# Direct tiles and last projections as floating filler in a convolution pipeline on TensorE

## The chip, the cores and the metric

One Trainium2 chip, one of its cores. The metric is the device time of one execution in microseconds (us). A dilated causal convolution with a gate and an output projection is computed; every engine runs a fixed list of instructions in order, made at build time by a small list scheduler inside the kernel, from modelled durations.

TensorE is PE in the profile (PEld: its weight loads), VectorE is DVE, ScalarE is ACT, SyncE is SP (it issues the DMAs).

## The reference, cut to what matters

```python
B, T, D, K = (2, 16000, 144, 15)        # x [2,16000,144], w [15,144,288], w_o [144,144], all bf16
h = sum over i in 0..14 of  xp[:, pad - 2*i : pad - 2*i + T, :] @ w[i]     # dilation 2, causal
z = tanh(h[..., :144]) * sigmoid(h[..., 144:])
return z @ w_o
```

## The kernel before: the parts that matter

Time is cut into 128 segments of 250 steps; a "tile" is one step of all 128 segments. The first ten tiles are "direct": 15 matmuls over the first 128 channels, 2 over the other 16, that is 17 a tile. All the others come in 30 "units", which share sums and differences between taps: VectorE prepares differences, TensorE multiplies (items named S, X, V, Y, D), ScalarE copies partial sums inside PSUM and from PSUM to SBUF, VectorE adds them, the D matmuls finish the sum in PSUM, ScalarE applies tanh and sigmoid, VectorE multiplies (Z), a transposing DMA and a projection follow. In what follows D of unit n is its first D matmul, WA,DD in the profile.

Inputs of the units are staged: an engine copies them into one of two staging buffers (STA by VectorE, STB by ScalarE) and a DMA transposes that into XA or XB.

```python
NST = 2                                          # staging buffers
def load_xb(o):                                  # 16 remaining channels of eight tiles
    for h in range(2):
        g.add("act", <copy XBc -> STB[:, q, half h]>, w=[("STB", q, h)], dur=0.5, prio=2)      # q = o % NST
    g.add("sp", <dma_start_transpose XB <- STB>, r=[("STB", q, 0), ("STB", q, 1)], w=[("XB", s)], dma="xb", ...)
```

The scheduler models a DMA as landing DMA_LAT = 2.3 us after its bytes have passed at 280 kB per us. The scheduler hands out the eight banks of PSUM, the memory that TensorE writes its sums to, and it does so in the program's order:

```python
asks = [op for op in self.ops if op.alloc]       # every operation that wants a bank
def banks(op):
    if op is not asks[ai[0]]:                    # not its turn: wait
        return None
    ...
```

`prio` orders operations that could start at the same time (a smaller number goes first), and an operation is never placed before those in `soft`. An operation on TensorE that is "floating" may be pulled out of TensorE's program order when nothing else is ready; all others keep it. The direct tiles did not float. The last unit's odd tiles are not projected through a transposing DMA but by TensorE itself, in "ship pairs": four transposes into two banks, a copy by VectorE and one by ScalarE, four matmuls into a third bank, an eviction by ScalarE, a store.

```python
fill = [f for k in range(6, 10) for f in direct_parts(k)]
for f in fill[:FILL0]:                           # FILL0 = 20: all of them, before unit 0
    f()
...                                              # the 30 units
for o in (o0, o1):                               # the end
    project_some(o, (0, 2, 4, 6)); store_some(o, (0, 2, 4, 6), 2, 4, 0)
for dl in dls:                                   # four ship pairs, each with two stores
    ship_pair(o0, o1, dl)                        # transposes and projection floating=True
    for o in (o0, o1):
        store_some(o, (dl,), 2, 1, dl)
```

Of the kernel before, what the change touches and what calls it, by code (L numbers as in the profile page):

```python
# [72 lines left out]
class _Graph:  # L73
# [58 lines left out]
    def run(self, hint):  # L132
# [36 lines left out]

        asks = [op for op in self.ops if op.alloc]  # L170
        ai = [0]

        def banks(op):
            if op is not asks[ai[0]]:
                return None
            got, used = [], set()
            for bk in op.alloc:
                c = [b for b in range(0, 8, bk.n) if all(bopen[x] and x not in used for x in range(b, b + bk.n)) and (bk.pin is None or bk.pin == b)]
                if bk.n == 1:
                    c = [b for b in c if not bopen[b ^ 1] or (b ^ 1) in used] or c  # L180
                if not c:
                    return None
                b = min(c, key=lambda b: (max(bfree[b:b + bk.n]), b))
                used.update(range(b, b + bk.n))
                got.append(b)
            return got
# [5 lines left out]
        while n < len(self.ops):  # L192
# [39 lines left out]
            else:  # L232
                op.end = st + op.dur + TAIL[op.eng]
            ai[0] += 1 if op.alloc else 0
            for bk, b0 in zip(op.alloc, got or ()):
# [92 lines left out]
def _conv_wavenet_kernel(nc, x, w, w_o, out):  # L328
# [38 lines left out]
    BANK_O = 6  # L367
    FILL0 = 20
    LAG = 2
# [3 lines left out]
    with contextlib.ExitStack() as st:  # L373
# [368 lines left out]
        def finish(bk, z0, z1):  # L742
            s = ts_n[0] % NTS
            ts_n[0] += 1

            def th(a):
                return a.activation(TS[:, s, 0, :, :], both(bk, 0, D), ACT.Tanh)  # L747

            def sg(a):
                return a.activation(TS[:, s, 1, :, :], both(bk, D, D), ACT.Sigmoid)  # L750
            g.add("act", [th, sg], r=[bk], w=[("TS", s)], frees=[bk], dur=2 * t_act(2 * D), prio=0)

            def gt(v):
                dst = bass.AP(Z[:].tensor, (z0[0] * 8 + z0[1]) * D, [[NZ * 8 * D, NP], [((z1[0] - z0[0]) * 8 + z1[1] - z0[1]) * D, 2], [1, D]])
                return v.tensor_tensor(dst, TS[:, s, 0, :, :], TS[:, s, 1, :, :], ALU.mult)  # L755
            g.add("dve", gt, r=[("TS", s)], w=[("Z",) + z0, ("Z",) + z1], dur=t_tt(2 * D))

        wor_keys = [("WORp", dl, part) for dl in range(8) for part in range(2)]
# [3 lines left out]
        def ship_pair(o0, o1, dl):  # L762
# [9 lines left out]
            g.add("pe", fns, r=[("Z", zs[0], dl), ("Z", zs[1], dl), "ID"], alloc=[pa, pb], dur=0.24, floating=True)  # L772
            g.add("dve", lambda v: v.tensor_copy(zt(q, 0, 256), PSb[:, pa.b * 1024:pa.b * 1024 + 256]), r=[pa], w=[("ZTL", q, 0), ("Xr", 0)], frees=[pa], dur=0.21)
            g.add("act", lambda a: a.activation(zt(q, 256, 256)[0:DB, :], PSb[0:DB, pb.b * 1024:pb.b * 1024 + 256], ACT.Copy), r=[pb], w=[("ZTL", q, 1)], frees=[pb], dur=0.29)
            bo = _Bank()
            fns = []
            for i in range(2):
# [7 lines left out]
                                                PS[:, bo.b * 512:bo.b * 512 + 2 * D].rearrange("p (a b) -> p a b", a=2), ACT.Copy),  # L785
                  r=[bo], w=[("OS", s0, dl), ("OS", s1, dl)], frees=[bo], dur=t_act(2 * D))
            for s in (s0, s1):
                if s in last_store:
                    op.deps.add(last_store[s])

        def store_some(o, dls, step, n, d0):
            os_ = o % NO

            def f(e):
                src = bass.AP(OS[:].tensor, (os_ * 8 + d0) * D, [[NO * 8 * D, NP], [step * D, n], [1, D]])
                dst = bass.AP(out_t, (KD + 8 * o + d0) * D, [[L * D, NP], [step * D, n], [1, D]])
                return e.dma_start(dst, src)
            g.add("sp", f, r=[("OS", os_, d) for d in dls], w=[], dur=0.5, dma="st", nbytes=NP * n * D * 2)

# [8 lines left out]

        def project(o, gi):
            a, c = GROUPS[gi]  # L810
# [4 lines left out]
            for blk in range(a, c + 1):  # L815
# [3 lines left out]
                def f(t, q0=q0, n=q1 - q0 + 1, blk=blk, wi=wi, first=(blk == a)):  # L819
# [3 lines left out]
                fns.append(f)  # L823
            g.add("pe", fns, r=[("ZT", zt)] + wor_keys, alloc=[bk], dur=0.1255 + 0.1227 * (c - a - 1))
            op = g.add("act", lambda e: e.activation(OS[:, os_, a:c, :].rearrange("p e d -> p (e d)"), PS[:, bk.b * 512:bk.b * 512 + (c - a) * D], ACT.Copy),  # L825
                       r=[bk], w=[("OS", os_, d) for d in range(a, c)], frees=[bk], dur=t_act((c - a) * D), prio=1)
            if os_ in last_store:
# [10 lines left out]
        def project_some(o, dls):  # L838
            zt, os_ = o % NZT, o % NO
            for part in (dls[:2], dls[2:]):  # L840
                bk = _Bank()

                def mk(bk=bk, part=part):
                    out = []
                    for i, dl in enumerate(part):
                        for k in range(2):
                            out.append(lambda t, i=i, dl=dl, k=k: t.matmul(PS[:, bk.b * 512 + i * D:bk.b * 512 + i * D + D], lhsT=ZT[:, zt, dl + k, :], rhs=WOR[:, 2 * dl + k, :],
                                                                           start=(i == 0 and k == 0), stop=True, skip_group_check=True))
                    return out
                g.add("pe", mk(), r=[("ZT", zt)] + wor_keys, alloc=[bk], dur=0.063 * 2 * len(part))  # L850
                op = g.add("act", lambda e, bk=bk, part=part: e.activation(bass.AP(OS[:].tensor, (os_ * 8 + part[0]) * D, [[NO * 8 * D, NP], [2 * D, len(part)], [1, D]]),
                                                                           PS[:, bk.b * 512:bk.b * 512 + len(part) * D].rearrange("p (a b) -> p a b", a=len(part)), ACT.Copy),
                           r=[bk], w=[("OS", os_, d) for d in part], frees=[bk], dur=t_act(len(part) * D))
                if os_ in last_store:
                    op.deps.add(last_store[os_])
# [185 lines left out]

        def direct(k, b, pi, t0, t1):
            e = H + k
            g.add("pe", region(b, [(lambda e_=e - DIL * i: xa_tile(e_)) for i in range(t0, t1)], [(lambda i_=i: WA[:, i_, :]) for i in range(t0, t1)], t0 == 0),
                  r=[("XA", aslot(o)) for o in sorted(set(oct_of(e - DIL * i)[0] for i in range(t0, t1)))] + [("WA", pi)], dur=(t1 - t0) * MM, **({"alloc": [b.bk]} if t0 == 0 and k % 2 == 0 else {"w": [b.bk]}))

        def direct_b(k, b):
            e = H + k
            g.add("pe", region(b, [lambda: xb_tile(e), lambda: xb_tile(e - 2)], [lambda: WB[:, 0, :], lambda: WB[:, 1, :]]),
                  r=[("XB", bslot(-1)), ("XB", bslot(0)), ("WB", 0), ("WB", 1)], w=[b.bk], dur=2 * MM)  # L1050

# [5 lines left out]
        load_xchunk(0).deps.add(wa_op)  # L1057
        dp = [_Bank(2 * i if i < 3 else None, 2) for i in range(5)]
        db = [_Half(dp[k // 2], k % 2) for k in range(10)]
# [4 lines left out]
        for pi, (t0, t1) in enumerate(wa_pieces):  # L1064
            for k in range(6):
                direct(k, db[k], pi, t0, t1)
        for k in range(6):
            direct_b(k, db[k])
            if k % 2:
                finish(dp[k // 2], zdir(k - 1), zdir(k))  # L1070

        def direct_parts(k):
            out = [lambda pi=pi, t0=t0, t1=t1: direct(k, db[k], pi, t0, t1) for pi, (t0, t1) in enumerate(wa_pieces)]

# [5 lines left out]

        fill = [f for k in range(6, 10) for f in direct_parts(k)]
        for f in fill[:FILL0]:
            f()
        fill = fill[FILL0:]
        load_xa(1)
# [88 lines left out]
        todo_p = []  # L1174
        shipped = False
        for t in range(-reach, NUN):
# [4 lines left out]
            for name, off in pattern:  # L1181
# [11 lines left out]
                if not 0 <= u < NUN:  # L1193
                    continue
                if t < 0 and fill:
                    fill.pop(0)()
                if name[0] == "G":
# [4 lines left out]
                if name[0] == "D":  # L1202
# [6 lines left out]
                    elif done_d[u] == 4 and u == NUN - 2:  # L1209
                        for o in (o0, o1):  # L1210
                            ship(o, (0, 2, 4, 6))
            if fill and t == -1:
                for f in fill:
                    f()
                fill = []
            if not fill and not shipped:
                ship(-1, (6, 7))
                ship(0, range(8))
                shipped = True
        for x in todo:  # L1220
            project(*x[:2])
        m, r, o0, o1 = octs(NUN - 1)
        for o in (o0, o1):
            project_some(o, (0, 2, 4, 6))
            store_some(o, (0, 2, 4, 6), 2, 4, 0)
        dorder = [x for x, _ in pattern if x[0] == "D"]
        dls = [{"D00": 7, "D01": 5, "D10": 3, "D11": 1}[x] for x in dorder]
        for dl in dls:
            ship_pair(o0, o1, dl)
            for o in (o0, o1):  # L1230
                store_some(o, (dl,), 2, 1, dl)

# [79 lines left out]
```

## Time and profile before

| | before |
|---|---|
| median of its runs beside the change | 353.55 us (353.21 to 353.84, 4 runs) |
| profiled execution | 354.46 us, span 352.7 us, mean granted clock 0.98 |
| TensorE, VectorE, ScalarE busy | 332.1, 301.9, 259.6 us |
| first direct matmul / D of unit 0 / D of unit 29 / end | 15.18 / 50.37 / 334.87 / 352.7 us |

The table of windows of the kernel before gives, for a stretch of the span, its length and then busy time and count of PE, PEld, DVE, ACT, POOL, the granted TensorE clock, the DMA share and GB/s:

```profile
45.00:50.00 5.00, 1.40 (x10) 0.90 (x10) 2.55 (x5) 2.39 (x5) 0.00 (x0) 0.83 1.13 207
50.00:60.00 10.00, 9.59 (x59) 6.68 (x59) 6.09 (x17) 5.76 (x15) 0.00 (x0) 0.74 0.44 139
...
120.00:140.00 20.00, 19.94 (x165) 14.94 (x164) 19.28 (x42) 16.99 (x43) 0.00 (x0) 1.00 0.72 153
```

In the body (last line) TensorE has no time left. At 45 to 50 us it works for 1.40 us of 5 and then, up to 60 us, runs at a mean clock of 0.74 with 59 matmuls in 10 us where the body has 82.

The timeline of TensorE, kernel before, around the start of unit 0 (start, length, engine, line, operation, tiles, shapes, count; in brackets how long the engine idled before it and what ended that):

```profile
33.92 2.00 PE L726 MATMUL PS<-WA,XA 128*128 128x288 bf16 x15
...
36.01 0.41 PE L726 MATMUL PS<-WT,DU 128*128 128x288 bf16 x2
37.95 0.42 PE L726 MATMUL PS<-WS,GU 128*128 128x288 bf16 x2 [1.54 <-ACT PS L875]
...
46.78 0.66 PE L726 MATMUL PS<-WD,DD 128*128 128x288 bf16 x4 [2.60 <-ACT PS L875]
...
50.37 0.90 PE L726 MATMUL PS<-WA,DD 128*128 128x288 bf16 x3 [2.19 <-DVE PS L1017]
51.06 0.45 PE L726 MATMUL PS<-WB,BF 128*128 128x288 bf16 x1
```

WA,XA is the last direct tile; unit 0 starts behind them at 36.0 us and waits. The chain of waits of the same kernel shows what stood behind the 2.60 us:

```profile
39.75 5.50 DMA XB<-STB
...
45.28 1.15 ACT STB L653 x2
46.42 0.31 ACT PS L875
...
46.78 0.68 PE PS L726 x4
```

ScalarE's copy for TensorE (L875) was ready to run, but stood behind a staging copy (L653) that waited for a staging buffer whose transpose landed after 5.50 us.

The end of the kernel before, timeline of TensorE: the first transpose (L770) of the first three ship pairs and the first projection (L778) of the first two.

```profile
340.96 0.22 PE L770 MATMUL PS<-ID,Z 128*128 128x128 bf16 x1
...
342.41 0.24 PE L778 MATMUL PS<-WOR,Xr 128*128 128x144 bf16 x1 [0.76 <-ACT Xr L774]
...
343.07 0.23 PE L770 MATMUL PS<-ID,Z 128*128 128x128 bf16 x1
...
344.25 0.23 PE L778 MATMUL PS<-WOR,Xr 128*128 128x144 bf16 x1 [0.47 <-ACT Xr L774]
...
344.90 0.23 PE L770 MATMUL PS<-ID,Z 128*128 128x128 bf16 x1
```

One pair after the other, each with its wait for the copies, although the transposes of the next could have filled it.

### The profile page before, as it was taken

To read this page: it belongs to the slowest core of one execution; us is meant where nothing else is said; L and a number is where in the kernel's file an instruction comes from. 1 tells how busy PE (TensorE), PEld (TensorE's weight loads), DVE (VectorE), ACT (ScalarE), POOL (GpSimd) and SP (SyncE) were. 2 spreads that over 40 slices of the span, in tenths; PEclk is the share of its full clock that TensorE was granted. 3 is DMA by queue.
4 is the path that set the end of the run, shared out by engine and by line. 5 is a ranking of instruction groups with operands and counts; after the bars stand their busy time and mean duration, and the time that the engine had idled before them with its cause. 6 is when DMAs were issued, how large, how long until landed. Compare 5 with 4: busy or idle time off the path is not lost.

```text
span 352.7 us, 7129 instructions
## 1 busy us (share of the span) xinstructions
PE 332.1 (94%) x2736; PEld 249.2 (71%) x2736; DVE 301.9 (86%) x658; ACT 259.6 (74%) x630; POOL 17.9 (5%) x30
## 2 busy tenths in 40 slices
PE   8799649999999999999999999999999999999984
PEld 8777426677777777777767777777777777777752
DVE  1999548999998999999999999998989989886630
ACT  3235637878887878879887878888787777777762
POOL 8830000000000000000000000000000000000000
PEclk9999978999999999999999999999999999999995
DMA  8789994578958587674758495561734260412351
GB/s 215 242 129 208 190 242 83 103 170 178 220 99 195 123 174 149 132 155 134 150 103 187 108 194 128 108 148 36 135 55 103 63 103 33 102 67 45 76 150 34
DMA packets 112573, 46.46 MB, mean 132 GB/s; under 512 B 103886, under 2 KB 106367, under 8 KB 112541
## 3 DMA queue, kind: packets, MB, share of 16 engines
q1 hardware_dynamic: 112025, 45.68, 61.3%
q0 software_dynamic: 512, 0.33, 0.4%
q8 instruction: 21, 0.34, 0.4%
q14 instruction: 11, 0.09, 0.1%
q10 hardware_dynamic: 4, 0.01, 0.0%
HBM read 11.82 MB, written 9.22 MB: 60 GB/s over the span
## 4 chain that ended last, share of the span: by engine, by line
PE 77%; ACT 9%; DMA 6%; DVE 5%; issue 1%; POOL 0%; DVEq 0%; POOLq 0%
PE PS L726 66%; PE PS L821 7%; DMA XB<-STB 6%; ACT STB L653 3%; ACT TS L747 2%; DVE Xp L996 2%; ACT TS L750 1%; PE PS L539 1%; ACT UX L944 1%; ACT PS L875 1%; DVE PS L1008 1%; DVE WC L614 1%; PE PS L778 1%; DVE V L672 0%; PE PS L780 0%
## 5 line engine op out<-in xcount | busy, mean ns | idle before, releaser
L996 DVE TENSOR_TENSOR Xp<-PS,UX 128x576 f32<-128x576 f32 x90 | 65.3, 754 | 13.4 <-PE PS L726 12.7
L1008 DVE TENSOR_TENSOR PS<-PS,Xp 128x576 f32<-128x576 f32 x90 | 68.8, 765 | 5.5 <-PE PS L726 4.2
L726 PE MATMUL PS<-WA,GD 128*128 128x288 bf16 x360 | 70.7, 289 | 0.9 <-DVE PS L1008 0.9
L747 ACT ACTIVATE TS<-PS 128x288 f16<-128x288 f32 x125 | 51.8, 415 | 16.5 <-PE PS L726 14.5
L875 ACT ACTIVATE PS<-PS 128x288 f32<-128x288 f32 x120 | 45.5, 405 | 23.4 <-PE PS L726 23.4
L750 ACT ACTIVATE TS<-PS 128x288 f16<-128x288 f32 x125 | 51.7, 414 | 0.0
L944 ACT ACTIVATE UX<-PS 128x576 f32<-128x576 f32 x60 | 39.0, 651 | 16.7 <-PE PS L726 14.8
L653 ACT ACTIVATE STB<-XBc 128x512 bf16<-128x512 bf16 x60 | 36.6, 636 | 18.7 <-DMA XB<-STB 12.6
L726 PE MATMUL PS<-WS,GU 128*128 128x288 bf16 x210 | 44.2, 286 | 1.5 <-ACT PS L875 1.5
L755 DVE TENSOR_TENSOR Z<-TS 128x288 bf16<-128x288 f16 x125 | 38.2, 306 | 6.6 <-ACT TS L750 6.4
L726 PEld LDWEIGHTS PS<-WA,GD 128*128 128x128 bf16 x360 | 35.0, 99 | 11.4 <-DVE PS L1008 2.3
L825 ACT ACTIVATE OS<-PS 128x432 bf16<-128x432 f32 (+1 forms) x88 | 42.4, 489 | 0.8
L821 PE MATMUL PS<-WOR,ZT 128*128 128x144 bf16 (+1 forms) x322 | 42.3, 254 | 0.0
L726 PE MATMUL PS<-WB,XB 128*128 128x288 bf16 x140 | 37.6, 286 | 0.0
L726 PE MATMUL PS<-WB,BE 128*128 128x288 bf16 x120 | 34.7, 289 | 0.0
L726 PE MATMUL PS<-WB,BF 128*128 128x288 bf16 x120 | 34.7, 289 | 0.0
L726 PE MATMUL PS<-WD,DD 128*128 128x288 bf16 x180 | 31.9, 287 | 2.8 <-ACT PS L875 2.8
L726 PE MATMUL PS<-WA,DD 128*128 128x288 bf16 x180 | 31.6, 293 | 2.4 <-DVE PS L1017 2.2
L821 PEld LDWEIGHTS PS<-WOR,ZT 128*128 128x128 bf16 x322 | 28.0, 98 | 6.1 <-ACT OS L825 0.6
L726 PE MATMUL PS<-WC,V 128*128 128x288 bf16 x180 | 30.6, 286 | 0.0
L726 PE MATMUL PS<-WT,DU 128*128 128x288 bf16 x120 | 25.1, 291 | 1.0 <-DVE Xp L996 0.8
L726 PEld LDWEIGHTS PS<-WS,GU 128*128 128x128 bf16 x210 | 20.3, 98 | 7.3 <-ACT PS L875 2.1
(89 smaller groups left out, 523.3 us busy)
## 6 DMA issues: line engine op xcount, KB each, us to landing
Xr<-in_x_dram SPq DMA_DIRECT2D x15, 576.0 KB, 4.2
out_dram<-OS SPq DMA_DIRECT2D x29, 288.0 KB, 2.4
WA<-in_w_dram SPq DMA_DIRECT2D x3, 288.0 KB, 5.1
ZT<-Z SPq DMA_TRANSPOSE x32, 3.8
Xp<-in_x_dram SPq DMA_DIRECT2D x2, 252.0 KB, 5.3
XA<-STA SPq DMA_TRANSPOSE x30, 3.3
XB<-STB SPq DMA_TRANSPOSE x30, 3.2
Xp<-in_x_dram SPq DMA_DIRECT2D x1, 441.0 KB, 4.2
```

The lines of the kernel that those rows point to most:

```text
L539: g.add("pe", [lambda t: t.matmul(PS[:, BANK_O * 512:BANK_O * 512 + 128], lhsT=ID[:], rhs=ONES[:], start=True, stop=True)] * n, r=["ID", " ...
L653: return v.activation(STB[:, q, 4 * h:4 * h + 4, :], src, ACT.Copy)
L726: return lambda t: t.matmul(bank(bk.b), lhsT=lhs(), rhs=rhs(), start=start, stop=True, skip_group_check=True)
L747: return a.activation(TS[:, s, 0, :, :], both(bk, 0, D), ACT.Tanh)
L750: return a.activation(TS[:, s, 1, :, :], both(bk, D, D), ACT.Sigmoid)
L755: return v.tensor_tensor(dst, TS[:, s, 0, :, :], TS[:, s, 1, :, :], ALU.mult)
L821: return t.matmul(PS[:, c0:c0 + n * D], lhsT=ZT[:, zt, blk, :], rhs=WOR[:, wi:wi + n, :].rearrange("p a b -> p (a b)"), start=first, stop= ...
L825: op = g.add("act", lambda e: e.activation(OS[:, os_, a:c, :].rearrange("p e d -> p (e d)"), PS[:, bk.b * 512:bk.b * 512 + (c - a) * D], A ...
L875: g.add("act", lambda e: e.activation(bank(bk.b + 1), bank(bk.b), ACT.Copy), w=[bk], dur=t_act(N2), prio=0)
L944: g.add("act", lambda e: e.activation(UX[:, k, u % NU, :, :], both(X, 0, N2), ACT.Copy), r=[X], w=[("UX", k, u % NU)], frees=[X], dur=t_ac ...
L996: g.add("dve", lambda v, k=k, wi=wi, vb=vb, us=us: v.tensor_tensor(wslot(wi), both(vb, 0, N2), UX[:, k, us, :, :], ALU.add), r=[vb, ("UX", ...
L1008: return v.tensor_tensor(both(d, 0, N2), src, wslot(wi), ALU.add)
```

## The change

Intent: (a) make the last four direct tiles filler, put by the scheduler wherever TensorE waits in unit 0; (b) let the last projections and ship pairs float as well, two ship pairs before the last projections, evictions of those by VectorE; (c) six stores at the end instead of ten. Cut to its core:

```diff
-        asks = [op for op in self.ops if op.alloc]
+        asks = [op for op in self.ops if op.alloc and not op.floating]
-            if op is not asks[ai[0]]:
+            if not op.floating and op is not asks[ai[0]]:
-    FILL0 = 20
+    KF = 6
         def direct(k, b, pi, t0, t1, after=None):        # direct_b likewise
-            g.add("pe", region(...), ...)
+            g.add("pe", region(...), floating=k >= KF, prio=2 if k >= KF else 1, soft=(after,), ...)
-        def project(o, gi):
+        def project(o, gi, last=False):                  # last: floating, prio 3, evicted by "dve"
         def project_some(o, dls):
-                g.add("pe", mk(), ...);                 op = g.add("act", ...)
+                g.add("pe", mk(), ..., floating=True, prio=3);  op = g.add("dve", ...)
+        for dl in dls[:2]: ship_pair(o0, o1, dl)
+        for dl in dls[:2]: store_both(o0, o1, dl)
         for o in (o0, o1):
             project_some(o, (0, 2, 4, 6)); store_some(o, 0)
-        for dl in dls:
+        for dl in dls[2:]:
             ship_pair(o0, o1, dl)
-            for o in (o0, o1): store_some(o, (dl,), 2, 1, dl)
+            store_both(o0, o1, dl)
```

(Cut: the copies and evictions of a ship pair also get the highest priority; the bank pairs of the direct tiles are fixed, and in the scheduler the last two direct tiles start only after ScalarE has begun with tanh of the first two.)

More of the change, by code (lines that the diff above doesn't have):

```diff
@@ L233, in run @@
                 op.end = st + op.dur + TAIL[op.eng]
-            ai[0] += 1 if op.alloc else 0
+            ai[0] += 1 if op.alloc and not op.floating else 0
             for bk, b0 in zip(op.alloc, got or ()):
@@ L750, in sg @@
                 return a.activation(TS[:, s, 1, :, :], both(bk, D, D), ACT.Sigmoid)
-            g.add("act", [th, sg], r=[bk], w=[("TS", s)], frees=[bk], dur=2 * t_act(2 * D), prio=0)
+            op = g.add("act", [th, sg], r=[bk], w=[("TS", s)], frees=[bk], dur=2 * t_act(2 * D), prio=0)
             def gt(v):
@@ L756, in finish @@
             g.add("dve", gt, r=[("TS", s)], w=[("Z",) + z0, ("Z",) + z1], dur=t_tt(2 * D))
+            return op
         wor_keys = [("WORp", dl, part) for dl in range(8) for part in range(2)]
@@ L772, in ship_pair @@
             g.add("pe", fns, r=[("Z", zs[0], dl), ("Z", zs[1], dl), "ID"], alloc=[pa, pb], dur=0.24, floating=True)
-            g.add("dve", lambda v: v.tensor_copy(zt(q, 0, 256), PSb[:, pa.b * 1024:pa.b * 1024 + 256]), r=[pa], w=[("ZTL", q, 0), ("Xr", 0)], frees=[pa], dur=0.21)
-            g.add("act", lambda a: a.activation(zt(q, 256, 256)[0:DB, :], PSb[0:DB, pb.b * 1024:pb.b * 1024 + 256], ACT.Copy), r=[pb], w=[("ZTL", q, 1)], frees=[pb], dur=0.29)
+            g.add("dve", lambda v: v.tensor_copy(zt(q, 0, 256), PSb[:, pa.b * 1024:pa.b * 1024 + 256]), r=[pa], w=[("ZTL", q, 0), ("Xr", 0)], frees=[pa], dur=0.21, prio=0)
+            g.add("act", lambda a: a.activation(zt(q, 256, 256)[0:DB, :], PSb[0:DB, pb.b * 1024:pb.b * 1024 + 256], ACT.Copy), r=[pb], w=[("ZTL", q, 1)], frees=[pb], dur=0.29, prio=0)
             bo = _Bank()
@@ L785, in ship_pair @@
                                                 PS[:, bo.b * 512:bo.b * 512 + 2 * D].rearrange("p (a b) -> p a b", a=2), ACT.Copy),
-                  r=[bo], w=[("OS", s0, dl), ("OS", s1, dl)], frees=[bo], dur=t_act(2 * D))
+                  r=[bo], w=[("OS", s0, dl), ("OS", s1, dl)], frees=[bo], dur=t_act(2 * D), prio=0)
             for s in (s0, s1):
@@ L789, in ship_pair, with store_some, store_both, f @@
                     op.deps.add(last_store[s])
-        def store_some(o, dls, step, n, d0):
+        def store_some(o, d0):
             os_ = o % NO
             def f(e):
-                src = bass.AP(OS[:].tensor, (os_ * 8 + d0) * D, [[NO * 8 * D, NP], [step * D, n], [1, D]])
-                dst = bass.AP(out_t, (KD + 8 * o + d0) * D, [[L * D, NP], [step * D, n], [1, D]])
+                src = bass.AP(OS[:].tensor, (os_ * 8 + d0) * D, [[NO * 8 * D, NP], [2 * D, 4], [1, D]])
+                dst = bass.AP(out_t, (KD + 8 * o + d0) * D, [[L * D, NP], [2 * D, 4], [1, D]])
                 return e.dma_start(dst, src)
-            g.add("sp", f, r=[("OS", os_, d) for d in dls], w=[], dur=0.5, dma="st", nbytes=NP * n * D * 2)
+            g.add("sp", f, r=[("OS", os_, d0 + 2 * i) for i in range(4)], w=[], dur=0.6, dma="st", nbytes=NP * 4 * D * 2)
+        def store_both(o0, o1, d0):
+            s0, s1 = o0 % NO, o1 % NO
+            def f(e):
+                src = bass.AP(OS[:].tensor, (s0 * 8 + d0) * D, [[NO * 8 * D, NP], [(s1 - s0) * 8 * D, 2], [1, D]])
+                dst = bass.AP(out_t, (KD + 8 * o0 + d0) * D, [[L * D, NP], [8 * D, 2], [1, D]])
+                return e.dma_start(dst, src)
+            g.add("sp", f, r=[("OS", s, d0) for s in (s0, s1)], w=[], dur=0.7, dma="st", nbytes=NP * 2 * D * 2)
         def ship(o, dls):
@@ L823, in project, with ev @@
                 fns.append(f)
-            g.add("pe", fns, r=[("ZT", zt)] + wor_keys, alloc=[bk], dur=0.1255 + 0.1227 * (c - a - 1))
-            op = g.add("act", lambda e: e.activation(OS[:, os_, a:c, :].rearrange("p e d -> p (e d)"), PS[:, bk.b * 512:bk.b * 512 + (c - a) * D], ACT.Copy),
-                       r=[bk], w=[("OS", os_, d) for d in range(a, c)], frees=[bk], dur=t_act((c - a) * D), prio=1)
+            g.add("pe", fns, r=[("ZT", zt)] + wor_keys, alloc=[bk], dur=0.1255 + 0.1227 * (c - a - 1), floating=last, prio=3 if last else 1)
+            eng = "dve" if last else "act"
+            def ev(e):
+                dst, src = OS[:, os_, a:c, :].rearrange("p e d -> p (e d)"), PS[:, bk.b * 512:bk.b * 512 + (c - a) * D]
+                return e.tensor_copy(dst, src) if eng == "dve" else e.activation(dst, src, ACT.Copy)
+            op = g.add(eng, ev,
+                       r=[bk], w=[("OS", os_, d) for d in range(a, c)], frees=[bk], dur=t_ps((c - a) * D) if last else t_act((c - a) * D), prio=2 if last else 1)
             if os_ in last_store:
@@ L849, in mk @@
                     return out
-                g.add("pe", mk(), r=[("ZT", zt)] + wor_keys, alloc=[bk], dur=0.063 * 2 * len(part))
-                op = g.add("act", lambda e, bk=bk, part=part: e.activation(bass.AP(OS[:].tensor, (os_ * 8 + part[0]) * D, [[NO * 8 * D, NP], [2 * D, len(part)], [1, D]]),
-                                                                           PS[:, bk.b * 512:bk.b * 512 + len(part) * D].rearrange("p (a b) -> p a b", a=len(part)), ACT.Copy),
-                           r=[bk], w=[("OS", os_, d) for d in part], frees=[bk], dur=t_act(len(part) * D))
+                g.add("pe", mk(), r=[("ZT", zt)] + wor_keys, alloc=[bk], dur=0.063 * 2 * len(part), floating=True, prio=3)
+                op = g.add("dve", lambda e, bk=bk, part=part: e.tensor_copy(bass.AP(OS[:].tensor, (os_ * 8 + part[0]) * D, [[NO * 8 * D, NP], [2 * D, len(part)], [1, D]]),
+                                                                           PS[:, bk.b * 512:bk.b * 512 + len(part) * D].rearrange("p (a b) -> p a b", a=len(part))),
+                           r=[bk], w=[("OS", os_, d) for d in part], frees=[bk], dur=t_ps(len(part) * D), prio=2)
                 if os_ in last_store:
@@ L1040, in item_D, with direct @@
             finish(bk, (zslot(o0, dl), dl), (zslot(o1, dl), dl))
-        def direct(k, b, pi, t0, t1):
+        def direct(k, b, pi, t0, t1, after=None):
             e = H + k
             g.add("pe", region(b, [(lambda e_=e - DIL * i: xa_tile(e_)) for i in range(t0, t1)], [(lambda i_=i: WA[:, i_, :]) for i in range(t0, t1)], t0 == 0),
-                  r=[("XA", aslot(o)) for o in sorted(set(oct_of(e - DIL * i)[0] for i in range(t0, t1)))] + [("WA", pi)], dur=(t1 - t0) * MM, **({"alloc": [b.bk]} if t0 == 0 and k % 2 == 0 else {"w": [b.bk]}))
+                  r=[("XA", aslot(o)) for o in sorted(set(oct_of(e - DIL * i)[0] for i in range(t0, t1)))] + [("WA", pi)], dur=(t1 - t0) * MM, floating=k >= KF, prio=2 if k >= KF else 1, soft=(after,), **({"alloc": [b.bk]} if t0 == 0 and k % 2 == 0 else {"w": [b.bk]}))
         def direct_b(k, b):
@@ L1049, in direct_b @@
             g.add("pe", region(b, [lambda: xb_tile(e), lambda: xb_tile(e - 2)], [lambda: WB[:, 0, :], lambda: WB[:, 1, :]]),
-                  r=[("XB", bslot(-1)), ("XB", bslot(0)), ("WB", 0), ("WB", 1)], w=[b.bk], dur=2 * MM)
+                  r=[("XB", bslot(-1)), ("XB", bslot(0)), ("WB", 0), ("WB", 1)], w=[b.bk], floating=k >= KF, prio=2 if k >= KF else 1, dur=2 * MM)
         for b in range(6, 8):
@@ L1057, in _conv_wavenet_kernel @@
         load_xchunk(0).deps.add(wa_op)
-        dp = [_Bank(2 * i if i < 3 else None, 2) for i in range(5)]
+        dp = [_Bank(2 * i % 8, 2) for i in range(5)]
         db = [_Half(dp[k // 2], k % 2) for k in range(10)]
@@ L1066, in _conv_wavenet_kernel @@
                 direct(k, db[k], pi, t0, t1)
+        fin = []
         for k in range(6):
@@ L1069, in _conv_wavenet_kernel @@
             if k % 2:
-                finish(dp[k // 2], zdir(k - 1), zdir(k))
+                fin.append(finish(dp[k // 2], zdir(k - 1), zdir(k)))
         def direct_parts(k):
-            out = [lambda pi=pi, t0=t0, t1=t1: direct(k, db[k], pi, t0, t1) for pi, (t0, t1) in enumerate(wa_pieces)]
+            out = [lambda pi=pi, t0=t0, t1=t1: direct(k, db[k], pi, t0, t1, fin[0] if k >= 8 and t0 == 0 else None) for pi, (t0, t1) in enumerate(wa_pieces)]
             def last():
@@ L1079, in direct_parts @@
             return out + [last]
-        fill = [f for k in range(6, 10) for f in direct_parts(k)]
-        for f in fill[:FILL0]:
-            f()
-        fill = fill[FILL0:]
+        for k in range(6, 10):
+            for f in direct_parts(k):
+                f()
         load_xa(1)
@@ L1174, in _conv_wavenet_kernel @@
         todo_p = []
-        shipped = False
         for t in range(-reach, NUN):
@@ L1194, in _conv_wavenet_kernel @@
                     continue
-                if t < 0 and fill:
-                    fill.pop(0)()
                 if name[0] == "G":
@@ L1211, in _conv_wavenet_kernel @@
                             ship(o, (0, 2, 4, 6))
-            if fill and t == -1:
-                for f in fill:
-                    f()
-                fill = []
-            if not fill and not shipped:
+            if t == -1:
                 ship(-1, (6, 7))
                 ship(0, range(8))
-                shipped = True
         for x in todo:
-            project(*x[:2])
+            project(*x[:2], last=True)
         m, r, o0, o1 = octs(NUN - 1)
+        dorder = [x for x, _ in pattern if x[0] == "D"]
+        dls = [{"D00": 7, "D01": 5, "D10": 3, "D11": 1}[x] for x in dorder]
+        for dl in dls[:2]:
+            ship_pair(o0, o1, dl)
+        for dl in dls[:2]:
+            store_both(o0, o1, dl)
         for o in (o0, o1):
             project_some(o, (0, 2, 4, 6))
-            store_some(o, (0, 2, 4, 6), 2, 4, 0)
-        dorder = [x for x, _ in pattern if x[0] == "D"]
-        dls = [{"D00": 7, "D01": 5, "D10": 3, "D11": 1}[x] for x in dorder]
-        for dl in dls:
+            store_some(o, 0)
+        for dl in dls[2:]:
             ship_pair(o0, o1, dl)
-            for o in (o0, o1):
-                store_some(o, (dl,), 2, 1, dl)
+            store_both(o0, o1, dl)
         _ms = g.schedule()
```

## The prediction

> **What bounds the kernel now.** One core, profiled span 352.7 us. From about 60 to 332 us it runs at TensorE's pace: the table of windows gives TensorE 19.95 of 20 us busy in 120-140, 140-160 and 200-220 us, VectorE 19.28. The change leaves that body alone and acts on two ends.
>
> *Start.* In the timeline TensorE runs the ten direct tiles without a gap from 15.18 to 36.0 us; the last four (68 matmuls) take 27.68 to 36.0 = 8.3 us. Only then does unit 0 begin, and it stumbles: waits of 1.54, 0.85, 0.44, 2.60 us (on ScalarE copies) and 2.19 us (on VectorE's combine) until its first D matmul at 50.37 us: 7.6 us idle of 35.2. After the last two the granted clock falls (0.74 in 50-60 us): matmuls go out every 0.24 us instead of 0.12 from 50.4 to 54.7 us, about 2.1 us lost. That half clock after idling is as the Trainium skill, "TensorE: Matmul & The Clock Gate", Part 1, describes it.
>
> *End.* The last D matmuls issue until 339.3 us. The four last transposed tiles go strictly one after another: transposes 0.65 us, wait 0.45 to 0.76 us for two copies, projection 0.65 us; they start at 340.96, 343.07, 344.90, 347.09 us. The cause: banks are handed out in program order, so tile n+1 cannot transpose before tile n has a projection bank. The clock is 0.5 at the end. Ten stores take the queue from 341.6 to 350.7 us.
>
> **What the change does.** No matmul is removed. (a) The four direct tiles become filler with a bank rule of their own, so unit 0 can begin when its operands are there: the VectorE differences that it needs appear at 26 to 32.8 us. The filler (8.3 us) is about as large as the holes (7.6 us). If all fitted, D of unit 0 would begin at 42.5 us and the clock dip would go: 10 us at most. I expect about 6 us: 4.5 of idle, 1.5 of clock. VectorE did 27.9 us of work in those 35.2 us, so it can hardly go much faster; ScalarE's queue still blocks on staging copies that wait for transposing DMAs (2.1, 2.1, 2.7 us); the order is fixed at build time by modelled durations.
> (b) Floating projections and ship pairs no longer take banks in program order: the last four tiles overlap, two of them before the last D matmuls, in the 0.86 us wait at 337.7 us and later ones. TensorE still has 6.8 us of projections and transposes after the D work, and then bounds the end: last D about 339.5, last projection about 345.5, eviction 0.41, store and end 2.8 as now: about 348.5 instead of 352.7, some 4.5 us.
> (c) VectorE evictions (estimated 0.4 to 0.5 us each) and six stores instead of ten: both engines have room there; alone worth under 1 us.
>
> All of (a) and (b) is on the critical path, since the body passes any shift on.
>
> **Prediction.** 353.65 - 6 - 4.8 = 342.8 us; 8 in 10 between 338.5 and 347.5. Faster by over 2%: 0.83; within: 0.15; slower: 0.02.
>
> **What would show it.** First D matmuls of unit 0 (WA,DD) at 43 to 46 us; direct-tile matmuls scattered between 28 and 45 us; clock near 1.0 in 45-60 us; last D to end of span about 9 us instead of 13; transposes of two tiles adjacent.
>
> **What would make it wrong.** Waits on staging DMAs or VectorE that stay at their old clock times (start gains 2 us); filler executed ahead of the real holes; direct tiles holding a bank pair and starving unit 0; VectorE, 96% busy afterwards, giving the gain back before 120 us.

## The result, and the profile after

The change took 342.98 us (342.62 to 343.42, 4 runs) against 353.55 us. The ratio is 0.9702, 95% interval 0.9685 to 0.9719. A ratio is the mean time of one kernel's fast runs over that of the other's of the same rounds, so not quite the ratio of the medians.

The timeline of TensorE after the change, around unit 0:

```profile
27.23 0.41 PE L726 MATMUL PS<-WT,DU 128*128 128x288 bf16 x2
27.48 2.00 PE L726 MATMUL PS<-WA,XA 128*128 128x288 bf16 x15
29.31 0.41 PE L726 MATMUL PS<-WS,GU 128*128 128x288 bf16 x2
...
39.21 0.42 PE L726 MATMUL PS<-WV,V 128*128 128x288 bf16 x2 [0.92 <-DVE Xp L1011]
39.47 1.14 PE L726 MATMUL PS<-WA,XA 128*128 128x288 bf16 x8
41.34 0.42 PE L726 MATMUL PS<-WT,DU 128*128 128x288 bf16 x2 [0.73 <-ACT TS L750]
...
43.25 0.53 PE L726 MATMUL PS<-WA,DD 128*128 128x288 bf16 x3
```

Unit 0 (WT,DU) starts at 27.2 instead of 36.0 us, direct matmuls stand between its items, and D of unit 0 starts at 43.25 us with no wait before it. The windows of the changed kernel in the 15 us that follow:

```profile
45.00:60.00 15.00, 14.54 (x116) 10.80 (x117) 15.00 (x36) 11.67 (x30) 0.00 (x0) 1.00 1.05 210
```

The clock is 1.00. Then a part is lost again; the chain of waits of the changed kernel:

```profile
54.17 5.85 DMA XB<-STB
...
60.04 0.63 ACT STB L653
60.67 0.54 ACT UX L959
```

It is the pattern of before: ScalarE in front of a staging buffer whose transpose takes 5.85 us to land, with the copy UX behind it. TensorE then waits 0.89 us for UX and 1.13 us for VectorE's Xp (timeline of TensorE):

```profile
61.27 0.42 PE L726 MATMUL PS<-WV,V 128*128 128x288 bf16 x2 [0.89 <-ACT UX L959]
...
63.54 0.42 PE L726 MATMUL PS<-WT,DU 128*128 128x288 bf16 x2 [1.13 <-DVE Xp L1011]
```

The end, timeline of TensorE:

```profile
330.05 0.22 PE L771 MATMUL PS<-ID,Z 128*128 128x128 bf16 x1
...
331.80 0.42 PE L726 MATMUL PS<-WA,GD 128*128 128x288 bf16 x2
...
335.99 0.42 PE L862 MATMUL PS<-WOR,ZT 128*128 128x144 bf16 x4
336.25 0.23 PE L779 MATMUL PS<-WOR,Xr 128*128 128x144 bf16 x1
```

The first ship pair transposes (L771) before the last D matmuls (331.80), and no matmul of the end has a wait in brackets any more. The clock, 0.50 from 346 us on in the kernel before, stays at 1.00 until the last matmul.

The same milestones in both profiles give the account (a positive number is time saved):

| stretch | before | after | saved |
|---|---|---|---|
| span start to first direct matmul | 15.18 | 14.74 | 0.44 |
| to D of unit 0 | 35.19 | 28.51 | 6.68 |
| to D of unit 1 | 11.97 | 10.24 | 1.73 |
| to D of unit 2 | 10.04 | 11.99 | -1.95 |
| to D of unit 29 | 262.49 | 261.86 | 0.63 |
| to the end | 17.83 | 13.46 | 4.37 |
| span | 352.7 | 340.8 | 11.9 |

The first line has nothing to do with the change: the input loads set it, and over all profiles it lies between 14.20 and 15.32 us. The profiled run of before was also 0.9 us slower than its median, so the account sums to more than the medians' 10.6 us. How far two profiles of one list differ can be seen in the run with the end alone, below: up to 338 us its TensorE, VectorE and ScalarE have the lists of the kernel before, and its second line is 34.41 instead of 35.19. Over all profiles the stretch from D of unit 2 to D of unit 29 takes 261.64 to 263.39 us. A difference under about 1 us between two profiles therefore says little, except in the tail: in all eight profiles that have the change's end as it is, it lies within 0.03 us.

### The profile page after: what moved, and what is told of

It reads as the page before. It is cut to its first block, busy times and chain, and to the rows that moved or that the text cites. A ratio compares the mean times of both kernels' runs of the same rounds, so it can differ in the third digit from the quotient of the medians.

```text
span 340.8 us, 7123 instructions
## 1 busy us (share of the span) xinstructions
PE 327.4 (96%) x2736; PEld 246.3 (72%) x2736; DVE 303.3 (89%) x662; ACT 258.8 (76%) x626; POOL 17.5 (5%) x30
## 4 chain that ended last, share of the span: by engine, by line
PE 80%; DMA 8%; ACT 5%; DVE 5%; issue 1%; SPq 1%
PE PS L726 70%; PE PS L831 7%; DMA XB<-STB 6%; ACT STB L653 2%; DMA Xp<-in_x_dram 1%; DVE Xp L1011 1%; ACT UX L959 1%; ACT TS L747 1%; ACT TS L750 1%; DVE PS L1023 1%; DVE WC L614 1%; ACT PS L890 0%; DVE Z L755 0%; SPq L476 0%; PE PS L781 0%
## 5 line engine op out<-in xcount | busy, mean ns | idle before, releaser
L726 PE MATMUL PS<-WA,GD 128*128 128x288 bf16 x360 | 69.9, 286 | 0.3 <-DVE PS L1023 0.3
L726 PE MATMUL PS<-WA,DD 128*128 128x288 bf16 x180 | 30.8, 287 | 0.1
```

Of the source, the lines that this page charges most:

```text
L726: return lambda t: t.matmul(bank(bk.b), lhsT=lhs(), rhs=rhs(), start=start, stop=True, skip_group_check=True)
```

## The experiments

Four groups: is the gain the sum of two parts; what sets the gain at the start; what sets it at the end; and can the part that was given back be had. Twelve kernels ran, all gave the correct result. "Shift" is the start time of D of unit 29 against the kernel before (334.87 us), "tail" the time from there to the end.

### The two parts alone

Start alone: the changed kernel with ship_pair, projections, stores and the end's loop of the kernel before; only the direct tiles are exempt from the bank order.

> Start of the change alone (direct tiles float), with the end of the kernel before. Theory (two independent parts that the body passes on): it keeps the start's shift of 7.1 to 7.5 us and none of the end's 4.4, so 353.55 - 7 = 346.5 us (345.5 to 347.5), first D of unit 0 near 43 us, last D11 to end about 17.8 us as before. Rival (the gain is mostly the end, the start's shift is eaten later): 349 us or more.

Measured: 347.45 us, ratio 0.9848 (0.9792 to 0.9905); D of unit 0 at 43.77 us, shift 6.97 us, tail 18.0 us. By the ratio to the kernel before, that is 5.4 us saved (3.4 to 7.4).

End alone:

```diff
-    KF = 6
+    KF = 10        # all direct tiles in program order again
```

> End of the change alone: all ten direct tiles again in front of unit 0. Theory: 353.55 - 4.4 = 349.2 us (348.5 to 350), first D of unit 0 at 50 us, the clock dip after it back, last D11 to end about 13.5 us. Rival: below 347 us, the end is worth more than the traces say.

Measured: 348.42 us, ratio 0.986 (0.9824 to 0.9897); D of unit 0 at 49.06 us, D of unit 1 12.07 us later (so the clock dip is back), shift 1.21 us (the lists there are those of the kernel before, so this is variation), tail 13.44 us. By the ratio that is 5.0 us saved (3.6 to 6.2).

What follows: the parts add, as closely as these intervals can tell. The product of the two ratios is 0.971, the change's own ratio 0.970. The body passes the start's shift on, as the shift of 7.0 us with an unchanged tail shows.

### What sets the gain at the start

Half of the filler:

```diff
-    KF = 6
+    KF = 8         # two direct tiles float, two stay in front
```

> The change with only two direct tiles (34 matmuls, 4.2 us) as filler, two in front of unit 0. Theory (holes of unit 0 are filled by what filler there is): about 4.2 us of holes filled, half of the start's gain lost: 346 us (345 to 347.5), D of unit 0 near 46.5 us. Rival (the operands' and the staging's arrival set unit 0's pace, the filler only has to be out of the way): about 343 to 344 us as with four.

Measured: 343.17 us, ratio 0.9716 (0.9678 to 0.9755); D of unit 0 at 44.77, of unit 1 at 55.34, of unit 2 at 64.95 us; shift 7.35 us. My theory lost and the rival held: 34 matmuls of filler do what 68 do. The full filler is 1.5 us ahead at D of unit 0 (43.25) and 0.5 us behind at D of unit 2 (65.48). Holes are not a fixed 7.6 us into which filler is poured; two units later something else sets the pace. (Whether the tiles had to float at all, or a fixed place between the items of unit 0 would have done, was not run.)

Useless filler: the end of the change, direct tiles in front, and matmuls on zeros that nobody reads.

```diff
-    KF = 6
+    KF = 10
+        for _ in range(40):                      # second version: 18
+            bk = _Bank()
+            g.add("pe", [<matmul of zeros into bk>] * 2, alloc=[bk], frees=[bk], floating=True, prio=5, soft=(lastdir,), ...)
```

> End of the change, direct tiles in front as before, and 80 useless matmuls (9.8 us, zeros into a free bank, result never read) as filler behind them: the holes are filled with nothing of use. Theory (idling drops the clock, worth 1.7 to 2.1 us): D of unit 0 stays at 50 to 51 us, clock near 1.0 in 50-60 us, D of unit 0 to D of unit 1 10.2 instead of 12.0 us, about 1.5 us faster than the run with the end alone: 347.7 us (347 to 348.5). Rival (the slow stretch after 50 us is not due to idling): the same 349.2 us or slower, clock still 0.75 in 50-60 us.

Measured: 349.2 us, ratio 0.9888 (0.9867 to 0.9909), no faster than the end alone. D of unit 0 at 49.19, of unit 1 10.14 us later, clock 1.00 in 50 to 60 us: so the clock part of the expectation came, the time did not. The run is confounded: 44 of the 80 matmuls stood behind D of unit 0 and cost time there. The second version has 36, all in front of it.

> As the run with 80 useless matmuls, but only 36 of them, all of which stand in front of unit 0's first D matmul; the other 44 stood behind it and cost TensorE time there (up to 5.4 us), which confounded that run. Theory (without idling no half clock, and the body passes the 1.9 us on): D of unit 0 near 49.2 us, D of unit 1 10.1 us later, and the 1.8 us kept to the end: 346.5 us (346 to 347.3) against 348.4 with the end alone. Rival (what the clock gives is taken back by ScalarE's staging waits within two units, as in the change itself): D of unit 1 early, but from unit 2 on no earlier than with the end alone: 348 to 349 us.

Measured: 347.81 us, ratio 0.9833 (0.9799 to 0.9868), between the two forecasts. Windows of this run, and the same stretch of the run with the end alone:

```profile
42.00:52.00 10.00, 8.36 (x64) 5.94 (x64) 7.41 (x15) 5.01 (x12) 0.00 (x0) 1.00 0.93 227
```

```profile
42.00:52.00 10.00, 5.57 (x34) 3.53 (x32) 5.20 (x10) 3.10 (x7) 0.00 (x0) 0.76 0.98 229
```

Counted from the first direct matmul (to leave out the input loads), D of unit 0, 1, 2 and 29 come at 34.39, 44.93, 55.49 and 317.13 us; with the end alone at 34.41, 46.48, 56.53 and 319.01 us. So useless work in the holes takes the half clock away: idling is its cause, as the Trainium skill's "TensorE: Matmul & The Clock Gate", Part 1, has it. In the trace it is worth 1.55 us at once, of which 0.5 us is lost again by unit 2. At unit 29 it is 1.9 us, but 0.8 us of that arose in the body, within what profiles vary there. The times of the two kernels, 347.81 and 348.42 us, were taken in different rounds and their ratios' intervals overlap, so the worth in time is not resolved.

### What sets the gain at the end

Banks in program order again, for everything that floats except the direct tiles:

```diff
+        self.free_ask = floating and prio == 2          # direct tiles only
-        asks = [op for op in self.ops if op.alloc and not op.floating]
+        asks = [op for op in self.ops if op.alloc and not op.free_ask]
```

> The change, but the floating operations of the end must again ask for banks in program order (direct tiles stay exempt). Theory (bank order made the last four tiles serial): most of the end's 4.4 us is lost: 346 to 347.5 us, transposes of tile n+1 only after tile n's projection was handed its bank. Rival (the new order of the lists and the priorities do it, banks do not matter): 343 us.

Measured: 348.8 us, ratio 0.9868 (0.9825 to 0.9911), more than the 346 to 347.5 us expected; tail 18.76 us: all of the end's 4.4 us is lost and 0.9 us more. (The profiled run, at 349.97 us, was the slowest of the four; the fastest took 347.04 us. The 0.9 us more agrees with what the clock costs: it is 0.50 in 337 to 345 us, and the sixteen partial projections take 1.89 us where they took 1.00 us before the change.) Timeline of TensorE in this run:

```profile
335.75 0.23 PE L772 MATMUL PS<-ID,Z 128*128 128x128 bf16 x1
...
336.92 0.29 PE L780 MATMUL PS<-WOR,Xr 128*128 128x144 bf16 x1 [0.47 <-ACT Xr L776]
...
339.72 0.31 PE L772 MATMUL PS<-ID,Z 128*128 128x128 bf16 x1
...
341.22 0.28 PE L780 MATMUL PS<-WOR,Xr 128*128 128x144 bf16 x1 [0.55 <-ACT Xr L776]
```

The pairs are serial again, with everything else of the change in place. So without lifting the bank order the end gains nothing. Whether lifting it is enough, without the new order of the lists and the new priorities, was not run.

VectorE's evictions undone:

```diff
-                op = g.add("dve", <tensor_copy>, ..., dur=t_ps(...), prio=2)
+                op = g.add("act", <activation Copy>, ..., dur=t_act(...), prio=2)
```

> The change with the four last partial projections evicted by ScalarE again. Theory (the engine does not matter, TensorE bounds the end): within 0.5 us of the change, 342.7 to 343.5 us. Rival (VectorE evictions take ScalarE off the end's chain): 1 to 2 us slower.

Measured: 344.64 us, ratio 0.9763 (0.9733 to 0.9793), tail 14.56 us, 1.10 us longer than the change's. The expectation of 0.5 us was wrong. The timeline shows how: with four more evictions on ScalarE, the scheduler places the last ship pair alone behind all the others.

```profile
338.24 0.23 PE L771 MATMUL PS<-ID,Z 128*128 128x128 bf16 x1
...
339.47 0.29 PE L779 MATMUL PS<-WOR,Xr 128*128 128x144 bf16 x1 [0.47 <-ACT Xr L775]
...
339.92 0.30 PE L779 MATMUL PS<-WOR,Xr 128*128 128x144 bf16 x1
```

In the change that pair's transposes stand beside the third pair's and the wait is filled. The rest of the difference in time (half a microsecond by the medians, 1 us by the ratios) lies before the end, where the instruction lists are the same; it is variation.

Ten stores again:

```diff
-            store_both(o0, o1, dl)
+            for o in (o0, o1): store_one(o, dl)
```

> The change with ten end stores instead of six. Theory: the last pair's second store is issued about 0.4 us later, so up to 0.5 us slower: 343.0 to 343.5 us. Rival (the queue is the end's bound): 1.5 us or more slower.

Measured: 344.08 us, ratio 0.9753 (0.9726 to 0.978), tail 13.95 us, so 0.5 us longer than the change's, as expected. The time lies above the 343.0 to 343.5 us expected; the rest of its 1.1 us (1.8 us by the ratios) is again not the edit's: TensorE, ScalarE and VectorE have exactly the lists of the change here, and D of unit 0 still came 0.7 us later, in a run in which ScalarE's longest wait for a staging buffer was 5.0 us instead of 2.6. Start alone, bank order, ScalarE evictions and ten stores all share the change's order up to the end; with the change itself that makes five profiles of the same start. D of unit 29 lies between 327.34 and 328.94 us in them, and the stretch from D of unit 1 to D of unit 2 is 11.98 to 12.79 us in all five: the loss there is no accident.

### Can the given-back part be had?

A third staging buffer, the direct test, does not fit: the last buffer needs 6,912 B and 3,360 B are left. Instead the scheduler's model was told that the transposes land later, so that it orders ScalarE's list otherwise.

```diff
-                op.end = dma_free + DMA_LAT
+                op.end = dma_free + DMA_LAT + (2.0 if op.dma in ("xa", "xb") else 0.0)
```

> The change, with the scheduler's model of the two staging transposes 2 us slower, so that ScalarE's staging copies stand later in its order; nothing else. Theory (what was given back, 1.95 us between D of unit 1 and D of unit 2, is ScalarE standing in front of a staging buffer whose transpose has not landed, because the model lands it too early): 341 to 342.5 us, ScalarE's wait for XB<-STB (5.8 us in 27-120 us) down to 2 us or less. Rival (VectorE, busy throughout, takes the gain back): unchanged, 342.7 to 343.5 us.

Measured: 339.83 us (339.61 to 340.39), ratio 0.9625 (0.9606 to 0.9643): faster than both kernels, and better than the 341 to 342.5 us expected. VectorE's work is the same, so the rival is out. (It did not run in the change's rounds; the two ratios to the kernel before, 0.9625 and 0.9702, put it at 0.992 of the change.) Waits of the changed kernel between 27 and 70 us, the first line of its answer (who waited for whom, us in total, times, longest):

```profile
ACT STB L653 <- DMA XB<-STB: 5.8, 3, 2.6
```

In this run that line is gone, and TensorE's waits in the same window are only these:

```profile
PE PS L726 <- DVE Xp L1011: 0.8, 2, 0.4
...
PE PS L726 <- ACT TS L750: 0.3, 1, 0.3
...
PE PS L726 <- ACT PS L890: 0.3, 1, 0.3
```

That is 1.4 us instead of the change's 4.6 us (2.5 + 0.9 + 0.7 + 0.3 + 0.2). The difference of 3.2 us agrees with what the run gained: D of unit 29 comes 3.14 us earlier, counted from the first direct matmul (309.46 against 312.60 us). D of unit 1 to D of unit 2 takes 10.22 us instead of 11.99, so what was given back there is had. But that is 1.8 us only; D of unit 0 already comes 2.9 us earlier (25.60 against 28.51 us), which the theory did not say. Of this, 0.7 us goes back before unit 1, since seven direct matmuls now stand behind D of unit 0, and 0.9 us in the body.

Which of the two transposes matters was tried by giving the 2 us to one alone.

> The change with the 2 us in the scheduler's model only on the XB transposes, whose staging copies ScalarE does. Theory (ScalarE standing behind a staging buffer in flight is the whole cause of what the change left in the start): 340 us (339.5 to 341), ScalarE's wait for XB<-STB in 27-120 us under 1 us. Rival (the XA transposes, staged by VectorE, or the mere reshuffle matter as much): 341.5 to 343.5 us.

Measured: 341.44 us, ratio 0.9656 (0.9621 to 0.9691); ScalarE's wait for XB<-STB 0.9 us in 27 to 120 us. The wait went as expected, the time did not: it misses 339.5 to 341 us, and its interval overlaps the change's (0.9685 to 0.9719), so a gain is not resolved. The theory that ScalarE's wait is the whole cause is not borne out.

> The same with the 2 us only on the XA transposes, whose staging copies VectorE does. Theory: the six staging copies at the head of ScalarE's list stay, so its wait for XB<-STB stays at 4 to 6 us in 27-120 us and the time at 342 to 343.5 us. Rival: 340 to 341 us.

Measured: 340.9 us, ratio 0.9632 (0.9592 to 0.9672); ScalarE's wait for XB<-STB 0.4 us. This expectation failed: I had looked at the head of ScalarE's list, which stays, but the lists further down change too, and the wait went away here as well. So the pair of runs does not single out one transpose, and the intervals of the two overlap. What all three have in common is that ScalarE's wait for XB<-STB falls from 5.8 us to at most 0.9, and that D of unit 29 comes 0.9 (XB alone), 2.4 (XA alone) and 3.1 us (both) earlier, counted from the first direct matmul. At D of unit 2 the leads are 2.5, 3.5 and 4.0 us, since D of unit 1 to D of unit 2 takes 9.59, 9.74 and 10.22 us instead of 11.99; the body then takes 1.5, 1.1 and 0.9 us more than in the change's profile. Only with XA in the correction does D of unit 0 come earlier (2.1 us with XA alone, 0.3 us later with XB alone). XB<-STB also lands sooner: its median from issue to landing in 15 to 70 us is 4.5 us in the change and 3.3 us in the first of the three runs. How much is the place in ScalarE's list and how much the less crowded transposes stays open.

Last, the same correction in the kernel before:

> The kernel before (direct tiles in front, end as before), with the model correction of 2 us on both transposes. Theory (half of unit 0's stumble in the kernel before is ScalarE behind staging buffers too: its 2.6 us hole ended with such a copy): the 2.6 us hole at 44 us goes, the 2.2 us one stays, so no idling long enough for the half clock: 350 us (348.5 to 351.5). Rival (the direct tiles in front alone make the stumble): 353 to 354 us.

Measured: 349.84 us, ratio 0.9897 (0.9861 to 0.9933), as expected: the 2.60 us wait is 0.24 us here, D of unit 0 comes at 46.40 us. One part of the expectation failed, about the clock. Timeline of TensorE in this run, and its windows:

```profile
43.84 0.29 PE L726 MATMUL PS<-WB,XB 128*128 128x288 bf16 x1
46.40 0.67 PE L726 MATMUL PS<-WA,DD 128*128 128x288 bf16 x3 [2.28 <-DVE PS L1017]
```

```profile
47.00:48.00 1.00, 1.00 (x6) 0.62 (x5) 0.47 (x2) 0.00 (x0) 0.00 (x0) 0.50 1.05 176
```

The one wait of 2.28 us, with only one of 0.24 us in the 3 us before it, was enough for the half clock.

## Why the prediction was right

The total was 342.8 us and came out at 342.98; the two parts were 6 and 4.8 us. Where the gain comes from was right in both; that the total fits to 0.2 us is luck, as errors of the start cancel.

- *Where the change acts, and that the body passes it on.* Right: the shift of the start alone is 6.97 us at unit 29 with the tail of before, and the two parts' ratios multiply to the whole.
- *Start, about 6 us (4.5 of idle, 1.5 of clock).* The sum is right, its composition is not. The stretch up to D of unit 0 became 6.68 us shorter, more than the 4.5, and the clock gave 1.73; but 1.95 us went back at once between units 1 and 2. 6.68 + 1.73 - 1.95 = 6.5 us. So about 2 us too little in one term was made up by a loss that no term had. The prediction's reserve against the full 10 us named ScalarE's staging copies and VectorE. The staging copies are what the chain shows in the stretch from unit 1 to unit 2, and the loss there is gone in all three runs with later landings in the model. But it is also gone (9.61 us) with half of the filler, where ScalarE still waits 5.3 us for XB<-STB, but before D of unit 0. So it matters where that wait falls; that it is all of the loss is not shown.
- *"The filler (8.3 us) is about as large as the holes (7.6 us)."* As an explanation of the gain this failed. Half of the filler gives the same time: two of the four tiles may stand in front of unit 0. The lead of 1.5 us at D of unit 0 that the other two buy is gone by D of unit 2, the stretch in which the change's chain has ScalarE's staging copy.
- *Where it would show.* D of unit 0 at 43.25 us (43 to 46 forecast), direct matmuls from 27.5 to 44.6 us, clock 1.00 in 45 to 60 us. The last D matmuls end at 332.7 us, 8.1 us before the end, where about 9 were forecast.
- *End, 4.5 us from bank order.* Right in mechanism and size: 4.37 us in the trace, and with the bank order put back the tail is longer than before the change. Not all of it is overlap, though. The waits that went add up to 3.0 us (0.86 + 0.76 + 3 x 0.47). The half clock that went with them is, by an estimate from the same timeline, worth another 0.8 us: without its wait, a ship pair takes 1.36 us at full clock, the last two took 1.7 and 1.9 us. The prediction saw that clock but has no term for it.
- *(c), "both engines have room there; alone worth under 1 us".* The stores are worth 0.5 us. The VectorE evictions (0.45 us each) are worth 1.1 us in the tail, by the order that the scheduler finds with them: without them the last pair stands alone. And half of (c) does not exist: the branch for the last full projections is never taken. The page's group of those evictions is the same in both kernels, first before, then after:

```profile
L825 ACT ACTIVATE OS<-PS 128x432 bf16<-128x432 f32 (+1 forms) x88 | 42.4, 489 | 0.8
```

```profile
L839 ACT ACTIVATE OS<-PS 128x432 bf16<-128x432 f32 (+1 forms) x88 | 42.4, 488 | 0.8
```

All 88 stayed on ScalarE: the loop over the units has drained the list of projections before the new loop sees it. Only the four partial ones moved.
- *VectorE giving the gain back before 120 us.* Not seen: from unit 2 to unit 8 the shift moves only from 6.90 to 7.14 us. What was given back went earlier, between units 1 and 2.

## What to carry to other kernels

When a scheduler hands out a resource in program order, "floating" operations do not float; look for pairs of instructions that could overlap and never do, and ask what both must queue for. When filler moves a start forward, ask what the next queue in line does at the new time: here ScalarE, in its fixed order, stood in front of a staging buffer, and a later landing of the transposes in the build-time model was worth another 3 us without any change to the work. Give back in a later stage can hide whether a part of a change was needed at all, so test a part at half its size.

## What the Trainium skill lacked or had wrong

- "TensorE: Matmul & The Clock Gate", Part 1 and "Why this matters for your kernels", names gaps of about 3 to 3.4 us as what brings the half clock back. Here one wait of 2.28 us did (clock 0.50 afterwards, in the kernel before with the later-landing model). At the end of the kernel before the clock fell to 0.63 in 345 to 346 us and 0.50 after it, where no single wait of TensorE since 342 us was longer than 0.76 us; it had worked 0.59 to 0.77 of each us (partly on transposes; whether these count like other matmuls was not tried). The page's "A second HAM failure mode" knows such micro-idling in another kernel, but gives no measure of it.
- "DMA: Bandwidth & Descriptors", "Latency and other measured facts", gives the transposing DMA a bandwidth of 261 GB/s where the middle dimension is not contiguous, and "Anatomy of one DMA" a fixed cost of about 2.0 us; for the 262,144 B of one XB transpose that is an estimate of 3.0 us, with a fixed cost that is not of SyncE's path (next point). The trace has 3.2 us at best, 4.5 in the median and 5.8 at worst between 15 and 70 us of the changed kernel. The page has nothing on how far the landing of such a transpose spreads while other DMAs run; the chain of the change has ScalarE behind a late one (5.85 us).
- The fixed 2.0 us of "Anatomy of one DMA" is fitted to GpSimd's path. Stores of 36 KB issued by SyncE landed in 1.5 us (median of eight, kernel before); the page has no such fit for that path.
